# A planner that follows every engine decides which side work stands between the products

## The chip, the cores and the metric

One Trainium2 chip, one of its cores. The metric is the device time of one execution in microseconds (us), shorter being better. A core has a matrix engine (TensorE, PE in the rows; its weight loads are PEld), a vector engine (VectorE, DVE), a scalar engine (ScalarE, ACT) and GpSimd (POOL). SyncE (SP) issues the DMAs. Each engine works through its own list of instructions in order; semaphores tie the lists together. TensorE writes to PSUM, which has eight banks here, and the others read it from there.

## The reference

Attention over four batches and eight heads, then two gated feed-forward layers, in the reference's own types (the weights are 64-bit floats).

```python
# attention: q_l, k_l, v_l (4, 8, 512, 64); q_g, k_g, v_g (4, 8, 32, 64)
out_g = sm(scale * q_g @ k_all.T) @ v_all                 # 32 global rows see all 544
s_l = concat(scale * q_l @ k_g.T, where(|i - j| <= 32, scale * q_l @ k_l.T, -1e9))
out_l = sm(s_l) @ concat(v_g, v_l)                        # a band of 65, and the global keys
x = concat(out_g, out_l) as (2176, 512)
# layer 1: RMS norm, SiLU gate, d_ff 1536
xn = x / sqrt(mean(x * x) + 1e-6) * rms_g
y = (silu(xn @ w_gate) * (xn @ w_val)) @ w_out
# layer 2: sigmoid gate, weights of its own
out = (sigmoid(y @ w2_gate) * (y @ w2_val)) @ w2_out
```

## The kernel before

The 2176 rows are 17 tiles of 128 rows: 16 local tiles T = 0 to 15 and a last one of the four batches' global rows, called xG. They are kept in three parts q = 0, 1, 2 of 6, 6 and 5 tiles, as a high and a low half in f16 (`xhi`, `xlo`). The feed-forward layers are cut into 12 blocks g of 256 hidden columns: g = 0 to 5 are layer 1, g = 6 to 11 layer 2. Every product of f32 accuracy is three products of f16 (high by high, high by low, low by high).

**Attention** is a list `steps` of small steps: `st_q` and `st_k` turn the tile's queries and keys (four transposes each, ScalarE copies), `st_a1` writes a band mask and the scores into two PSUM banks (L809 and L816), `st_mx` and `st_ex` make the softmax, `st_a2` turns it (transposes, L747), `st_a3` multiplies by the values (L871), `st_nm`, `st_rm`, `rms_scale` norm it, `st_a4` and `st_a4b` turn it into `xhi` and `xlo`. `st_sg` and `st_g1` to `st_g3` do the global rows. `slot(u)` writes the steps of half a tile in the order of the list `ORDER`, with fixed lags between a tile's steps. Up to step n0 (four steps behind the third tile's `st_a4b`) a fixed plan runs them with the first weights between.

**Blocks 0 to 2** run on "chunks" of three tiles: `gv_mm` (48 products, L311) makes gate and value, `gv_post` multiplies them into `hhi`, `hlo` (t on VectorE at L334 to L340, hhi on ScalarE, hlo on GpSimd), and `out1` (24 products, L499) multiplies by the third weight and adds into `yacc`. Below, "a full product" is one of 128x384 of L311 or L499. `flush()` issues the `out1` of the chunk before, after the first half (24 products) of a chunk. `first` sets the order of the chunks of g = 0 and 1: the two blocks alternate as tiles come ready.

**Blocks 3 to 11** run on the parts q. `quad_gv` needs 7 instead of 8 sub-products of 2x2 blocks, which takes sums of the weights (`sums`) and of x (`x_combos`, `y_combos`; tiles xb, tt). A pair of products fills one of four PSUM pairs `p`, and VectorE adds it into G or V (L421). Block 6 is plain.

**Weights.** A weight n (three per block) is loaded as 64-bit words in two halves (`raw`, three buffers), turned to f32 by ScalarE (L139) and VectorE (a shift L151, the sign L154, the low bits L157), and split into a high half (ScalarE, L187) and a low half (VectorE, L190).

**What sets the order.** `tick(n)` stands behind every group of products. It counts: every `pace[1]`-th tick takes one lump from `w_jobs` (a lump is up to five weight instructions), every second or third one lump of `jobs` (the combos), and attention steps follow a rate from `due`, so that they are spread over the products of g = 0 and 1. `w_need` and `j_need` issue what is still missing when a block begins.

Of the kernel before, what the change touches and what calls it, by code (L numbers as in the profile page):

```python
# [1 line left out]

# [17 lines left out]
def tile_attention_moe_moe(  # L20
# [110 lines left out]
    def w_scale(n):  # L131

        if n >= NPC or not wide:
            return
        words = w_words.setdefault(n, [])
        if len(words) < 2:
            f = f_tile(n)[:, len(words)]
            words.append(raw_t.pop(0))
            nc.scalar.activation(out=f, in_=words[-1][:, :, 1].bitcast(F32), func=AF.Copy, scale=2.0 ** -112)  # L139

    def w_ahead(k):
        while w_pos[0] < min(k, 2 * NPC):
            w_load()

    def w_bits(n, j, k):

# [1 line left out]
        js = range(2) if j is None else [j]
        if k == 0:
            v = u if j is None else u[:, j]  # L150
            nc.vector.tensor_scalar(out=v, in0=v, scalar1=3, scalar2=None, op0=ALU.logical_shift_left)  # L151
        for j in js:
            if k == 0:
                nc.vector.scalar_tensor_tensor(out=u[:, j], in0=w_words[n][j][:, :, 1], scalar=-0x80000000, in1=u[:, j],  # L154
                                               op0=ALU.bitwise_and, op1=ALU.bitwise_or)
            else:
                nc.vector.scalar_tensor_tensor(out=u[:, j], in0=w_words[n][j][:, :, 0], scalar=29, in1=u[:, j],  # L157
                                               op0=ALU.logical_shift_right, op1=ALU.bitwise_or)

    def w_conv1(n):  # L160
        w_ahead(2 * n + (3 if wide else 2))
        w_scale(n)
        w_scale(n)
        if wide:
            w_bits(n, None, 0)

    def w_conv2(n):
        if wide:
            w_bits(n, None, 1)
            w_words.pop(n)  # L170
            w_ahead(2 * n + 5)
            w_scale(n + 1)

    def w_half(n, j):
        w_ahead(2 * n + (j + 3 if wide else 2))
        if wide:
            if len(w_words.get(n, [])) <= j:
                w_scale(n)
            w_bits(n, j, 0)
            w_bits(n, j, 1)  # L180
            w_scale(n + j)
            w_ahead(2 * n + j + 4)
            if j == 1:
                w_words.pop(n)
# [12 lines left out]
    def w_block(g):
        w_done[g] = [False, False]

        def mark(i):  # L200
            w_done[g][i] = True

        jobs = []

        def small(f):

            def f2():
                f()
                w_step()
            return f2  # L210

        def late():
            while w_late:
                w_lo(*w_late.pop())

        def conv(w):
            n = 3 * g + w
            if g < GS:
                return [lambda: (late(), w_half(n, 0)), lambda: w_half(n, 1)]
            return [lambda: (late(), w_conv1(n)), lambda: w_conv2(n)]  # L220

        def plain(w, dst):
            def f():
                hi, lo = dst()
                x = w_f.pop(3 * g + w)
                w_hi(x, hi)
                w_late.append((x, hi, lo))
                w_scale(3 * g + w + 1)
            return f

        if g < GS:
            def alloc():
                w_t[g] = [hp.tile([128, 2, 2, 2, DM], F16, tag="wgv", name="wgv"), None]

            jobs.append(small(alloc))
            for w in range(2):
                jobs += conv(w) + [plain(w, lambda w=w: [w_t[g][0][:, :, w, a] for a in range(2)])]
        else:
            def alloc():
                w_t[g] = [pb[1].tile([128, 2, 2, 7, 256], F16, tag="wc", name="wc", bufs=2), None]  # L240

            jobs.append(small(alloc))
            box = {}

            def sums(w):
                x = w_f[3 * g + w].rearrange("p j (a f) -> p (j a) f", a=2)
                sm = pb[1].tile([128, 3, 256], F32, tag="sm", name="sm")
                box[w] = x, sm
                ES[0].tensor_tensor(out=sm[:, 0], in0=x[:, 0], in1=x[:, 2], op=ALU.subtract)
                ES[1].tensor_tensor(out=x[:, 2], in0=x[:, 2], in1=x[:, 3], op=ALU.add)  # L250

            def sums2(w):
                x, sm = box[w]
                ES[2].tensor_tensor(out=sm[:, 1], in0=x[:, 2], in1=x[:, 0], op=ALU.subtract)
                ES[3].tensor_tensor(out=sm[:, 2], in0=x[:, 1], in1=sm[:, 1], op=ALU.subtract)

            def hi(w, i):
                w_hi(box[w][i], w_t[g][0][:, w, 0, (0, 4)[i]:(4, 7)[i]])

            def lo(w, i):  # L260
                a, b = (0, 4)[i], (4, 7)[i]
                w_lo(box[w][i], w_t[g][0][:, w, 0, a:b], w_t[g][0][:, w, 1, a:b])
                if i == 0:
                    w_f.pop(3 * g + w)

            for w in range(2):
                jobs += conv(w)
                if g == GP:
                    def parts(w=w):
                        return [w_t[g][0][:, w, a, 0:4].rearrange("p (j a) f -> p j (a f)", j=2) for a in range(2)]  # L270
                    jobs.append(plain(w, parts))
                else:
                    jobs += [lambda w=w: sums(w), lambda w=w: (sums2(w), hi(w, 0)), lambda w=w: (lo(w, 0), hi(w, 1)),
                             lambda w=w: (lo(w, 1), w_scale(3 * g + w + 1))]
            if g == GP:
                jobs.append(small(late))
        wgv_done = len(jobs)

        def alloc_o():
            w_t[g][1] = (hp if g < GS else pb[1]).tile([128, 2, 2, DM], F16, tag="wo", name="wo", bufs=2 if g < GS else 3)  # L280

        jobs += conv(2) + [small(alloc_o), plain(2, lambda: [w_t[g][1][:, :, a] for a in range(2)])]
        if g < GS:
            jobs.insert(wgv_done + 1, small(lambda: mark(0)))
        else:
            jobs.insert(wgv_done, small(lambda: mark(0)))
# [977 lines left out]
```

## Time and profile before

| | |
|---|---|
| median of 3 runs | 930.08 us (929.59 to 931.49) |
| the profiled execution | 930.12 us |
| its span, first to last instruction | 928.3 us |
| TensorE busy | 884.2 us, 95% of the span |
| VectorE, ScalarE, GpSimd busy | 644.8, 373.9, 298.3 us |
| mean granted clock of TensorE | 0.982 of 2.4 GHz |

The profiled execution's own time is 1.8 us over its span and equals the median of the runs. "Busy" counts a matmul from issue to the modelled end of its pipeline, so 95% doesn't mean that only 5% can be had; where matmuls follow each other at a steady pace, the pace is read from the start of one to the start of the next.

### The profile page before, as it was taken

What the parts mean: (1) busy time and instruction counts of PE and PEld (TensorE: products, weight loads), DVE (VectorE), ACT (ScalarE), POOL (GpSimd) and SP (SyncE); (2) the same over time, 40 slices, a digit from 0 to 9 for tenths busy, and PEclk for the clock granted to TensorE, in tenths of its full rate; (3) what the DMA queues carried; (4) which work ended last, traced back from release to release, by engine and by line L of the source; (5) the groups of instructions that cost most, each with busy time, mean ns of one, the idle gap of its engine ahead of it and who ended that gap; (6) DMA issues with size and microseconds to landing.
All of it is one profiled execution on the core that took longest, in us unless ns stands there. A gap on an engine that the chain in (4) does not pass through costs nothing.

```text
span 928.3 us, 19289 instructions
## 1 busy us (share of the span) xinstructions
PE 884.2 (95%) x8119; PEld 549.8 (59%) x8119; DVE 644.8 (69%) x907; ACT 373.9 (40%) x713; POOL 298.3 (32%) x344
## 2 busy tenths in 40 slices
PE   7678889999997999999999799999999999999998
PEld 4556566666674667666666466656556555556553
DVE  2967676446477787899957977738598566997352
ACT  3766666354453342343423444434344223423120
POOL 5544424223256661223221453242122203112120
PEclk9879999999997999999999999999999999999999
DMA  9987874331012111211201211101122011200102
GB/s 193 233 181 153 174 180 99 74 72 25 4 47 90 47 46 46 91 46 46 92 1 46 86 51 46 46 1 47 46 90 92 1 46 46 91 24 1 68 23 102
DMA packets 94183, 67.19 MB, mean 72 GB/s; under 512 B 59280, under 2 KB 84368, under 8 KB 94096
## 3 DMA queue, kind: packets, MB, share of 16 engines
q1 hardware_dynamic: 94096, 65.95, 26.8%
q8 instruction: 64, 1.05, 0.5%
q14 instruction: 23, 0.19, 0.1%
HBM read 52.17 MB, written 4.46 MB: 61 GB/s over the span
## 4 chain that ended last, share of the span: by engine, by line
PE 82%; DVE 10%; issue 3%; ACT 2%; DMA 1%; POOL 1%; SPq 1%; DVEq 0%; POOLq 0%; ACTq 0%
PE p L364 29%; PE p L521 13%; PE b L311 13%; PE p L499 7%; PE b L499 6%; PE p L462 5%; PE b L747 3%; PE b L816 2%; DVE wf L154 2%; PE b L871 2%; DVE wf L157 1%; DVE wf L151 1%; DVE G L421 1%; PE b L789 1%; DMA raw<-in_moe_w_gate_dram 1%
## 5 line engine op out<-in xcount | busy, mean ns | idle before, releaser
L364 PEld LDWEIGHTS <-wc 128*128 128x128 f16 x2016 | 197.4, 98 | 121.1 <-DVE G L421 4.8
L364 PE MATMUL p<-tt,wc 128*128 128x384 f16 (+1 forms) x1152 | 202.0, 319 | 5.9 <-DVE G L421 5.4
L364 PE MATMUL p<-xhi,wc 128*128 128x384 f16 (+1 forms) x576 | 156.3, 317 | 0.0
L401 POOL TENSOR_TENSOR h<-V,h 128x768 f16<-128x768 f32 (+1 forms) x48 | 80.4, 1696 | 235.5 <-ACT h L398 218.3
L311 PE MATMUL b<-xhi,wgv 128*128 128x384 f16 (+1 forms) x576 | 143.0, 319 | 0.0
L521 PE MATMUL p<-wo,h 128*128 128x512 f16 x612 | 133.4, 379 | 0.0
L499 PEld LDWEIGHTS <-wo 128*128 128x128 f16 x864 | 85.2, 99 | 58.4 <-issue 10.9
L311 PEld LDWEIGHTS <-wgv 128*128 128x128 f16 x864 | 83.2, 98 | 45.8 <-issue 1.9
L521 PEld LDWEIGHTS <-h 128*128 128x128 f16 x612 | 59.8, 98 | 71.1 <-POOL h L401 0.2
L311 PE MATMUL b<-xlo,wgv 128*128 128x384 f16 (+1 forms) x288 | 91.6, 318 | 0.4 <-DVE xlo L921 0.4
L364 PE MATMUL p<-xlo,wc 128*128 128x384 f16 (+1 forms) x288 | 91.4, 317 | 0.0
L481 DVE SCALAR_TENSOR_TENSOR ya<-p,ya 128x768 f32<-128x768 f32 (+3 forms) x42 | 42.3, 1017 | 60.6 <-PE p L521 48.2
L499 PE MATMUL b<-hhi,wo 128*128 128x384 f16 (+1 forms) x288 | 76.0, 330 | 7.4 <-ACT hhi L342 4.9
L428 ACT ACTIVATE sa<-p 128x384 f32<-128x384 f32 (+1 forms) x48 | 22.5, 469 | 132.7 <-PE p L364 119.9
L343 POOL TENSOR_TENSOR hlo<-t,hhi 128x384 f16<-128x384 f32 (+1 forms) x36 | 38.5, 1068 | 109.0 <-ACT hhi L342 109.0
L398 ACT ACTIVATE h<-V 128x1536 f16<-128x1536 f32 (+1 forms) x24 | 33.9, 1413 | 93.5 <-DVE V L397 93.5
L499 PE MATMUL p<-h,wo 128*128 128x384 f16 (+1 forms) x432 | 67.3, 317 | 0.0
L421 DVE TENSOR_TENSOR V<-p,V 128x768 f32<-128x768 f32 (+3 forms) x72 | 56.6, 787 | 12.1 <-PE p L364 9.3
L421 DVE TENSOR_TENSOR G<-p,G 128x768 f32<-128x768 f32 (+3 forms) x72 | 56.6, 785 | 8.6 <-PE p L364 6.2
L139 ACT ACTIVATE wf<-raw 128x512 f32<-128x512 f32 x72 | 48.4, 674 | 16.6 <-DMA raw<-in_moe_w_gate_dram 14.3
L157 DVE SCALAR_TENSOR_TENSOR wf<-raw,wf 128x512 int32<-128x512 int32 x72 | 53.8, 779 | 0.6
L154 DVE SCALAR_TENSOR_TENSOR wf<-raw,wf 128x512 int32<-128x512 int32 x72 | 52.4, 758 | 1.6
(137 smaller groups left out, 1296.0 us busy)
## 6 DMA issues: line engine op xcount, KB each, us to landing
raw<-in_moe_w_gate_dram SPq DMA_DIRECT2D x24, 512.0 KB, 4.0
raw<-in_moe_w_val_dram SPq DMA_DIRECT2D x24, 512.0 KB, 4.2
raw<-in_moe_w_out_dram SPq DMA_DIRECT2D x24, 512.0 KB, 3.9
vw<-vt SPq DMA_DIRECT2D x28, 260.0 KB, 5.1
k<-in_k_l_dram SPq DMA_DIRECT2D x16, 256.0 KB, 5.3
q<-in_q_l_dram SPq DMA_DIRECT2D x16, 256.0 KB, 4.5
vt<-in_v_l_dram SPq DMA_DIRECT2D x32, 128.0 KB, 5.0
out_dram<-ya SPq DMA_DIRECT2D x16, 256.0 KB, 2.3
```

The costliest lines, as they stand in the source:

```text
L139: nc.scalar.activation(out=f, in_=words[-1][:, :, 1].bitcast(F32), func=AF.Copy, scale=2.0 ** -112)
L154: nc.vector.scalar_tensor_tensor(out=u[:, j], in0=w_words[n][j][:, :, 1], scalar=-0x80000000, in1=u[:, j], op0=ALU.bitwise_and, op1=ALU.bi ...
L157: nc.vector.scalar_tensor_tensor(out=u[:, j], in0=w_words[n][j][:, :, 0], scalar=29, in1=u[:, j], op0=ALU.logical_shift_right, op1=ALU.bit ...
L311: nc.tensor.matmul(p[:, 0:n], wgv[:, j, gv, a, k * 128:(k + 1) * 128], x[xi][:, k, o:o + n], start=(i == 0), stop=(i == 11),)
L343: EH[3].tensor_tensor(out=lo, in0=t, in1=hi, op=ALU.subtract)
L364: nc.tensor.matmul(p, wc[:, w, a, wi, kt * 128:(kt + 1) * 128], r, start=(i == 0), stop=(i == 5))
L401: EH[j // 2].tensor_tensor(out=lo[:, i:i + 2], in0=vj[:, i - j:i - j + 2], in1=hi[:, i:i + 2], op=ALU.subtract)
L421: nc.vector.tensor_tensor(out=o, in0=p, in1=i, op=ALU.add)
L462: nc.tensor.matmul(gv[:, w], wc[:, w, a, c, (k % 2) * 128:(k % 2 + 1) * 128], x[q][:, k, h * n:(h + 1) * n], start=(i == 0), stop=(i == 11))
L481: nc.vector.scalar_tensor_tensor(out=ya, in0=p, scalar=1.0 / WS, in1=ya, op0=ALU.mult, op1=ALU.add)
L499: nc.tensor.matmul(p[:, i, 0:n], wo[:, j, a, d * 128:(d + 1) * 128], hh[:, j, ho:ho + n], start=(c == 0), stop=(c == 6 * len(gr) - 1),)
L521: nc.tensor.matmul(p[:, i], hh[:, j, (i0 + i) * 128:(i0 + i + 1) * 128], wo[:, j, a, :], start=(c == 0 and g == gr[0]), stop=(c == 5 and g ...
```

## The change

Every call to an engine goes through `Booked`, which issues it as before and also books it: an account holds when each engine is free (`now`), when each tile is written (`wrote`) and when a buffer is free again (`free0`), at costs written in the code. `tick` becomes two loops. `go_on` issues attention steps as long as the account says that the inputs of the next one are there. `give` issues single weight and combo instructions (`c_ops`, `s_ops`, `jobs`), the one due first ahead, while the account says that inputs are ready and the engine is less than `SLACK` (1 us; `ATT`, 0.5 us, during attention) behind TensorE. The lumps, `pace`, `due` and `MARGIN` are gone; `w_need` and `j_need` stay.

Four edits stand beside it: the chunks of block 0 all run before those of block 1 (`first`); once attention is over, `out1` is issued behind the second half of the next chunk (48 products) instead of the first; `st_sg` moves up in `ORDER`; the mask products take 64 rows (as the scores do) instead of 32, and their GpSimd set-up shrinks. The number of full products, quads, weights and sums is the same.

```diff
+    def book(key, outs, ins, cost, lat, port=False):
+        t = max([now[key]] + [wrote.get(tag_of(x), 0.0) for x in ins] + [free0.get(x.tensor.name, 0.0) for x in outs])
+        if port:
+            t = max(t, now["port"])
+            now["port"] = t + cost
+        now[key] = t + cost
...
+                    if key == "d":
+                        c = 75 + (0.52 if sb and len(data) < 2 and "axis" not in kw else 1.04) * n
+                    elif key == "a":
+                        c = 100 + 0.83 * n + 90 * (kw.get("bias") is not None) + 190 * ("accum_out" in kw)
...
+    EARLY = {"e": 100, "d": 500, "a": 500, None: 0}
+
+    def go_on():
+        while pos[0] < len(steps):
+            e, ins = needs(*steps[pos[0]])
+            t = max([0.0] + [wrote.get(tile_name(x), 0.0) for x in ins])
+            if t > now["e"] + EARLY[e]:
+                return
+            run_to(pos[0] + 1)
...
+    def fits(key, op):
...
+        sl = SLACK if pos[0] == len(steps) else ATT
+        t = max(now["e"], now[e]) + sl
+        if now[e] > now["e"] + sl or ins and any(wrote.get(tag_of(x), 0.0) > t for x in ins()):
+            return False
+        return free or ready.get(key, 0) <= t
...
     def tick(n):
-        pace[0] += 1
-        if jobs and pace[0] % pace[2] == 0:
-            i = min(range(len(jobs)), key=lambda i: (jobs[i][0][1], i))
-            jobs.pop(i)[1]()
-        if pace[0] % pace[1] == 0:
-            w_step()
-        t0 = clock[0]
-        clock[0] = t1 = t0 + n
-        if t0 < due[-1][0]:
-            rate = max((s - clock[1]) / (c - t0) for c, s in due if c > t0)
-            clock[1] += max(rate, 0.0) * n
-            run_to(int(clock[1]))
-
+        go_on()
+        give()
...
-    first = [(0, 0, 3), (0, 3, 3), (1, 0, 3), (1, 3, 3), (0, 6, 3), (1, 6, 3), (0, 9, 3), (1, 9, 3), (0, 12, 3), (0, 15, 2), (1, 12, 3), (1, 15, 2)]
...
+    first = [(0, 0, 3), (0, 3, 3), (0, 6, 3), (0, 9, 3), (0, 12, 3), (0, 15, 2), (1, 0, 3), (1, 3, 3), (1, 6, 3), (1, 9, 3), (1, 12, 3), (1, 15, 2)]
...
                 gv_mm(g, ch, j, 1)
+                if j == 1 and wi < len(work) - 1:
+                    flush()
                 gv_post(g, ch, j)
                 tick(ch[2])
-                if j == 0 and wi < len(work) - 1:
+                if j == 0 and wi < len(work) - 1 and pos[0] < len(steps):
                     flush()
...
-    ORDER = ['g1', 'a1', 'k', 'a2', 'mx', 'sc', 'q', 'g1x', 'sg', 'a3', 'a4', 'ex', 'a4b', 'nm', 'rm', 'g']
+    ORDER = ['g1', 'a1', 'sg', 'k', 'a2', 'mx', 'sc', 'q', 'g1x', 'a3', 'a4', 'ex', 'a4b', 'nm', 'rm', 'g']
```

Three places show what moves. In the changed kernel every booked instruction carries the line of the wrapper, L111. The first is TensorE in the attention of tile 10. Before, one step (four transposes of a tile's softmax, `s`) stands between groups of six full products of block 1:

```order
L311 MATMUL b_2428<-xhi0_73,wgv_1486 128x384
L747 MATMUL b_2495<-ident_82,s_2294 128x128 x4
L311 LDWEIGHTS wgv_1486
L311 MATMUL b_2504<-xhi0_73,wgv_1486 128x384
L311 LDWEIGHTS wgv_1486
L311 MATMUL b_2504<-xlo0_76,wgv_1486 128x384
```

In the changed kernel the steps behind the scores of tile 10 follow each other (transposes of s, q, the products by the values, transposes of x), and the next full product is one of block 0's `out1`:

```order
L111 MATMUL b_2537<-ident_82,s_2395 128x128 x4
L111 MATMUL b_2546<-ident_82,q_2142 128x128 x4
L111 MATMUL b_2555<-vw1_89,pt_2448 32x65 x16
L111 MATMUL b_2572<-ident_82,x_2268 128x128 x4
L111 LDWEIGHTS wo_1132
L111 MATMUL b_2583<-hhi_1579,wo_1132 128x384
```

From the scores of tile 5 to the transposes of xG, which are the last of attention, 606 full products stand on TensorE before and 234 after; tiles 9 to 15 have 366 and 84 of them. The attention steps between are the same. The 372 products moved behind attention.

The second place is VectorE where the sums of x and the weights meet the `t` of `gv_post`. Before, between two `t` in a row, thirteen instructions stand:

```order
L334 SCALAR_TENSOR_TENSOR t_4574<-b_4559,t_4574 128x384
L151 TENSOR_SCALAR wf_2310<-wf_2310 128x512
L154 SCALAR_TENSOR_TENSOR wf_2310<-raw_2241,wf_2310 128x512
L157 SCALAR_TENSOR_TENSOR wf_2310<-raw_2241,wf_2310 128x512
L616 TENSOR_TENSOR xb_4579<-xhi0_73,xlo0_76 128x768
L590 TENSOR_TENSOR xb_4579<-xb_4579 128x768
L190 SCALAR_TENSOR_TENSOR wgv_4553<-wf_2310,wgv_4553 128x2x512
L151 TENSOR_SCALAR wf_4584<-wf_4584 128x512
L154 SCALAR_TENSOR_TENSOR wf_4584<-raw_2312,wf_4584 128x512
L157 SCALAR_TENSOR_TENSOR wf_4584<-raw_2312,wf_4584 128x512
L590 TENSOR_TENSOR xb_4579<-xb_4579 128x384
```

(three more weight instructions, and then the next `t`). In the changed kernel a like place has nine, none of them a sum of x:

```order
L111 SCALAR_TENSOR_TENSOR t_4130<-b_4115,t_4130 128x384
L111 SCALAR_TENSOR_TENSOR wf_4064<-raw_3865,wf_4064 128x512 x2
L111 TENSOR_SCALAR wf_4064<-wf_4064 128x512
L111 SCALAR_TENSOR_TENSOR wf_4064<-raw_4044,wf_4064 128x512 x2
L111 TENSOR_SCALAR wf_4177<-wf_4177 128x512
L111 SCALAR_TENSOR_TENSOR wf_4177<-raw_4082,wf_4177 128x512 x2
L111 SCALAR_TENSOR_TENSOR wgv_4181<-wf_4064,wgv_4181 128x2x512
L111 SCALAR_TENSOR_TENSOR t_4214<-b_4149,t_4214 128x384
```

The third is VectorE in the last quad of block 5 (part 2), where layer 2's sums begin. Before, a sum of y (ya) and two weight instructions stand among the additions of G:

```order
L397 SCALAR_TENSOR_TENSOR V<-V,G 128x1536
L421 TENSOR_TENSOR G<-p,sa 128x2x320
L590 TENSOR_TENSOR ya_79<-ya_79 128x768
L157 SCALAR_TENSOR_TENSOR wf<-raw,wf 128x512 x2
L421 TENSOR_TENSOR G<-p,G 128x2x320
L421 TENSOR_TENSOR G<-p,G 128x320
```

In the changed kernel the additions of G follow each other:

```order
L111 SCALAR_TENSOR_TENSOR V<-V,G 128x1536
L111 TENSOR_TENSOR G<-p,sa 128x2x320
L111 TENSOR_TENSOR G<-p,G 128x2x320
L111 TENSOR_TENSOR G<-p,G 128x320
L111 TENSOR_TENSOR G<-p,G 128x2x320
L111 TENSOR_TENSOR ya_79<-ya_79 128x768
L111 TENSOR_TENSOR V<-p,sa 128x2x320
```

The weight instructions stand behind that quad's additions of V now.

## Rows read from the trace of the kernel before

**Rows 1.** The page: engines, and granted clock in 40 slices

```profile
PE 884.2 (95%) x8119; PEld 549.8 (59%) x8119; DVE 644.8 (69%) x907; ACT 373.9 (40%) x713; POOL 298.3 (32%) x344
...
PEclk9879999999997999999999999999999999999999
```

**Rows 2.** Windows between marks of attention: us, busy (x instructions), granted clock, DMA

```profile
17.01:60.50 43.49, 31.03 (x825) 23.50 (x819) 38.08 (x70) 28.23 (x82) 22.80 (x35) 0.84 0.94 215
60.50:110.84 50.34, 42.30 (x933) 30.47 (x930) 31.12 (x64) 32.53 (x99) 21.22 (x42) 0.93 0.84 171
110.84:212.80 101.96, 97.81 (x1646) 65.08 (x1646) 58.98 (x119) 56.82 (x162) 33.41 (x60) 1.00 0.45 104
212.80:251.59 38.79, 38.79 (x523) 25.58 (x523) 22.82 (x54) 15.17 (x37) 12.82 (x20) 1.00 0.07 17
251.59:928.30 676.71, 660.58 (x4044) 396.76 (x4041) 492.68 (x602) 234.25 (x318) 201.00 (x147) 0.99 0.15 52
```

**Rows 3.** Chain that ended last: a stretch of products without a wait

```profile
363.59 27.30 PE p L364 x168
```

**Rows 4.** TensorE's waits, 60.50 to 110.84: total us, times, longest

```profile
PE b L816 <- issue: 2.8, 1, 2.8
PE b L816 <- ACT kT L763: 1.7, 1, 1.7
PE b L747 <- DVE x L891: 1.1, 1, 1.1
PE b L871 <- issue: 0.8, 1, 0.8
PE b L959 <- ACT ptg L944: 0.7, 1, 0.7
PE b L747 <- DVE xlo L921: 0.7, 1, 0.7
PE b L311 <- DVE xlo L921: 0.4, 1, 0.4
```

**Rows 5.** Windows of 5 us in attention

```profile
27.00:32.00 5.00, 5.00 (x124) 3.77 (x124) 4.83 (x9) 4.38 (x16) 1.28 (x3) 0.61 0.65 143
32.00:37.00 5.00, 4.14 (x172) 3.27 (x169) 4.84 (x10) 5.00 (x15) 0.75 (x1) 1.00 1.21 286
...
62.00:67.00 5.00, 2.97 (x64) 2.41 (x66) 3.66 (x7) 2.92 (x12) 3.93 (x7) 0.80 0.93 173
67.00:72.00 5.00, 4.62 (x116) 3.51 (x117) 2.47 (x6) 3.24 (x10) 0.00 (x0) 0.86 0.64 152
```

**Rows 6.** TensorE's waits, 251.59 to 928.30

```profile
PE p L364 <- DVE G L421: 5.4, 3, 4.4
PE b L499 <- ACT hhi L342: 4.9, 2, 3.1
PE b L499 <- POOL hlo L343: 1.0, 2, 0.5
PE p L364 <- DVE V L421: 0.5, 1, 0.5
```

**Rows 7.** Windows around these waits

```profile
262.00:297.00 35.00, 29.26 (x193) 19.42 (x192) 28.62 (x36) 15.84 (x29) 18.52 (x13) 0.90 0.28 90
297.00:363.60 66.60, 66.44 (x430) 42.66 (x430) 49.43 (x72) 24.14 (x43) 39.76 (x32) 0.97 0.15 48
492.00:524.00 32.00, 26.98 (x171) 16.96 (x169) 28.86 (x32) 14.77 (x19) 10.08 (x6) 0.95 0.20 66
```

**Rows 8.** VectorE in order of time: two t of a chunk

```profile
268.27 0.56 DVE L334 SCALAR_TENSOR_TENSOR t<-b,t 128x384 f32<-128x384 f32 x1 [1.34 <-PE b L311]
...
279.69 0.55 DVE L334 SCALAR_TENSOR_TENSOR t<-b,t 128x384 f32<-128x384 f32 x1
```

**Rows 9.** VectorE and GpSimd in order of time, at the longest wait

```profile
513.87 4.17 DVE L157 SCALAR_TENSOR_TENSOR wf<-raw,wf 128x512 int32<-128x512 int32 x2
...
513.73 3.77 POOL L401 TENSOR_TENSOR h<-V,h 128x768 f16<-128x768 f32 x2 [8.84 <-ACT h L398]
```

**Rows 10.** Groups by form: the mask products

```profile
L809 PE MATMUL b<-mask,ident 32*32 32x256 bf16 x128 | 6.8, 290 | 0.0
```

More of the change, by code (lines that the diff above doesn't have):

```diff
@@ L143, in w_ahead, with w_give, w_shift @@
+    w_used = [0]
+    w_go = [False]
+    def w_give():
+        h = hist.get(("stg", "raw"), [])
+        while (wide and w_go[0] and w_pos[0] < 2 * NPC and w_pos[0] - w_used[0] < 3 and now["s"] < now["e"] + 1500
+               and (len(h) < 3 or last.get(h[-3], 0.0) < now["e"] + 500)):
             w_load()
-    def w_bits(n, j, k):
+    def w_shift(n, j):
         u = w_f[n].bitcast(I32)
[L148 to L169, printed above, removed]
[L170 to L184 removed]
+        v = u if j is None else u[:, j]
@@ L190, in w_lo @@
         nc.vector.scalar_tensor_tensor(out=lo, in0=f, scalar=WS, in1=hi, op0=ALU.mult, op1=ALU.subtract)
-    w_jobs = []
-    w_late = []
-    w_done = {}
-    def w_block(g):
-        w_done[g] = [False, False]
[L200 to L208, printed above, removed]
-                w_step()
[L210 to L237, printed above, removed]
-        else:
[L239 to L286, printed above, removed]
-        jobs.append(lambda: (late(), mark(1)))
-        w_jobs.extend(jobs)
@@ new lines, in tile_attention_moe_moe, with due_w, due_j @@
+    starts = {}
+    def due_w(ops):
+        x = ops[0]
+        left = sum(y.g == x.g and (y.w < 2) == (x.w < 2) for y in (*c_ops, *s_ops))
+        return starts.get((x.g, 0) if x.w < 2 else (group[x.g][-1], 1), now["e"] + 50000 * x.g) - STEP * left
+    def due_j(key):
+        q, k = key
+        left = sum(len(x[1]) for x in jobs if x[0] == key)
+        if k == 0:
+            t = starts[GP, q]
+        else:
+            t = min(t for (g, p), t in starts.items() if p == q and g not in (2, GP) and t > now["e"])
+        return t - STEP * left
@@ L575, in outs @@
             h_t.pop((g, key))
+            if key in (2, chunks_b[-1]) or g < 2 and key == last[g]:
+                wo_live.remove(g)
     jobs = []
-    EG = [nc.vector if c == "d" else nc.gpsimd for c in "ddpppppdpd"]
+    EGN = "ddpppppdpd"
+    EG = [nc.vector if c == "d" else nc.gpsimd for c in EGN]
     def combos(q, kt, b):
@@ L640, in tile_attention_moe_moe @@
     gB = const.tile([128, DM], F32, name="gB")
-    masks = [const.tile([128, 128], BF16, name=f"mask{i}") for i in range(3)]
+    mask = const.tile([128, 5, 32], BF16, name="mask")
     qgT = const.tile([128, NPR, B * SG], F32, name="qgT")
```

433 lines of the change are left out of this document (352 added, 81 removed).

## Prediction

> **What bounds the kernel now.** I read the page first, then windows between marks, then what TensorE waited for, then the other engines in order of time at the longest waits. The page shows TensorE at 95% and no other engine above 69% [rows 1], so the reader should ask where TensorE stands still or runs at a lower clock. No product is added or removed; only such losses can change the time.
>
> A price for products first: 168 of them, back to back, take 27.30 us [rows 3], 0.1625 us each for 128x384. The order says how many full products stand between two marks, so the rest of a window is attention with its losses. The marks are the mask of tile 5 (60.50), of tile 9 (110.84), of tile 15 (212.80) and the transposes of xG (251.59) [rows 2]:
> - Tile 5 to 9: 72 full products, 11.7 us of 50.34. Attention with its losses: 38.6 us for 4 tiles, 9.66 each.
> - Tile 9 to 15: 366 products, 59.5 us of 101.96. Attention: 42.5 us for 6 tiles, 7.1 each, at a granted clock of 1.00.
> - Tile 15 to xG: 168 products, 27.3 us of 38.79. Attention: 11.5 us.
>
> So attention is cheap on TensorE where many products stand between its steps, and dearer where few do. The waits of the dear stretch are listed: 4.6 us for ScalarE and VectorE (1.7 + 1.1 + 0.7 + 0.7 + 0.4) and 3.6 us "issue", in which nothing shown was waited for [rows 4]. The mean clock there is 0.93 [rows 2]; in the two windows from 62 to 72, where those for kT and x fall, the clock is 0.80 and 0.86 [rows 5], which is 5 x 0.20 + 5 x 0.14 = 1.7 us.
>
> Behind attention TensorE waits 5.4 + 4.9 + 1.0 + 0.5 = 11.8 us [rows 6], and the clock stands below full in the windows around: 35.0 x 0.10 + 66.6 x 0.03 + 32.0 x 0.05 = 7.1 us [rows 7]. Together 18.9 us. All of it is VectorE coming late, by itself or through ScalarE and GpSimd, which wait for its results.
>
> **The change, part by part.**
>
> *Waits behind attention.* The 4.9 and 1.0 us are `out1` waiting for hhi and hlo. VectorE has 11.4 us between two t (268.27 to 279.69) [rows 8], where TensorE needs 24 x 0.1625 = 3.9 us for the products behind them. Three edits work on this. Weights and sums go out one by one; in the changed order the like place holds 9 weight instructions and no sum of x. `out1` comes 48 products behind its last t, 7.8 us instead of 3.9. And attention ends 372 products earlier in the list, so the sums of x and the weights of blocks 1 to 4 have 372 x 0.1625 = 60.5 us more of products to hide behind. I take these 5.9 us of waits, and the 3.5 + 2.0 us of clock behind them, as gone.
>
> The 5.4 us are additions of G that came late. At the longest, two weight instructions at L157 took 4.17 us while GpSimd had 3.77 us of work on h over the same stretch [rows 9], and the additions of G stood behind them. In the changed order they stand behind that quad's additions of V instead, and the sum of ya behind G's. What that cost VectorE is not removed; it moves to a place where TensorE doesn't wait for it, if the four PSUM pairs give enough slack.
>
> The Trainium skill has a rule for this ("SBUF — State Buffer", the part on engine ports): VectorE with two SBUF inputs and GpSimd lock one port pair for a whole instruction, and the loser waits. The 4.17 us agree with it. By it the conflict goes wherever the two meet, so moving the weights could put it in another quad; that is one reason why I don't count the whole 18.9.
>
> What may stay: bounds 0 (every wait gone) and 18.9 us (none). The account prices VectorE at 75 ns plus 1.04 ns per element and books conflicts, so it lets a little too much through; a wait like the 4.4 us one with part of its clock may come back somewhere. I leave 3 us. **Gain behind attention: 15.9 us.**
>
> *Attention.* This term I am least sure of. From tile 5 to xG 234 full products stand instead of 606: 38.0 us. The account starts a step only when its inputs are (by its own clock) there, but it has little else to issue: block 0 alone feeds it. Per tile, 5 to 15 now hold 14 products (144 for 10 tiles), which is close to tile 5 to 9 before (18), not to 9 to 15 (61). So I start from the near row, 38.6 us for 4 tiles, and take off what a better order could avoid: 4.6 us of waits and the 1.7 us of clock, but not the "issue" waits. That leaves 32.3, **8.1 us per tile**; bounds 7.1 and 9.66. The stretch becomes 10 x 8.1 + 11.5 x 8.1/7.1 + 38.0 = 81 + 13.1 + 38.0 = 132.1 us. Before it took 191.1 us, of which 60.5 moved behind attention at full pace: 130.6. **Attention loses 1.5 us.** ScalarE and VectorE don't bound it at that: their busy time from tile 5 to 9 was 32.5 and 31.1 us for 4 tiles [rows 2], 8.1 and 7.8 per tile with 4 more products each, beside 8.1 + 14 x 0.1625 = 10.4 us.
>
> The Trainium skill speaks against denser attention ("TensorE: Matmul & The Clock Gate", Part 4): transposes don't count as activity for the clock the way products do. Here the trace doesn't follow it: the clock rose from 0.61 to 1.00 between 27 and 37 us, where only attention steps run [rows 5]. By the page the moved-together steps would run at the lower level, and the stretch would come out longer; the trace shows the low clock behind waits.
>
> *First 60 us.* The fixed plan stays; `st_sg` is earlier, one copy of pt stands behind the second tile's value copies on VectorE, and the weights come in half-lumps. VectorE bounds this part (38.08 of 43.49 us [rows 2]) and its instructions are the same. The most to gain is its idle time there, 43.49 - 38.08 = 5.4 us; for a loss I allow as much. Taken as nothing.
>
> *The mask.* 128 mask products are 6.8 us [rows 10], 8 per tile. If the 64-row form runs twice as many side by side it gains up to 3.4 us, if half as many it loses 6.8. I take nothing. GpSimd's shorter set-up lies ahead of the first scores, which wait for loads.
>
> *Sum.* 930.1 - 15.9 + 1.5 = 915.7, so **916 us**. The profiled execution (930.12) is the median of the runs, so no correction is due.
>
> **Rivals.**
> - *Attention stays cheap*, 7.1 us per tile: 71 + 11.5 + 38.0 = 120.5 us, a gain of 10.1; and with it only 1 us of the late waits returns, a gain of 17.9. 930.1 - 28.0 = **902 us**. For it: the account knows each step's inputs and the engines have room. Against: the cheap row had 61 products per tile.
> - *Attention starves TensorE* (the one that ends slower): with few products each wait is bare, the clock falls behind it, and a tile costs 9.66 us, as before between tile 5 and 9: 96.6 + 11.5 x 9.66/7.1 + 38.0 = 150.2 us, a loss of 19.6. 930.1 - 15.9 + 19.6 = **934 us**. It decides from (11.62 x t + 38.0) = 130.6 + 15.9, a tile cost of t = 9.3 us. For it: a measured row with nearly the same mix. Against: 6.3 of its 38.6 us come from the order that the change replaces.
> - *The late waits only move*: VectorE has the same work, and the additions of G wait at other quads for what stood at this one. Then 15.9 us of gain vanish and attention's small loss stays: **931 us**, about as before.
>
> **How the numbers follow.** Forecast 0.57 (908 to 925), attention cheap 0.22, starved 0.15, waits moved 0.06. Under 0.2% (1.9 us) a measurement of this kernel can't tell from no change. The last case spreads around no change: 0.01 faster, 0.05 the same. Faster: 0.57 + 0.22 + 0.01 = 0.80. Slower: 0.15. Same: 0.05. The range must leave out no more than 0.2: it reaches down to the cheap case, 901, and up to just below the starved one, 931.
>
> **What would show it.** The windows of the changed kernel should show 132 us between the masks of tile 5 and the transposes of xG, at a clock of 0.93 to 1.00; then no wait of TensorE over 3 us up to the end, the `out1` of blocks 1 and 2 without waits for hhi, and a clock of 1.00 in the stretch where the sums of x are made. L157 beside GpSimd's h may still take 4 us for two; TensorE should not wait behind it. Wrong would be: masks 12 us apart and more with waits for ScalarE in between (starved), or additions of G named in waits of several us (moved).

## The result and the profile after

The changed kernel takes **921.06 us** (median, 920.17 to 922.31), the kernel before 929.84 (928.73 to 931.49) beside it: a ratio of **0.9905 [0.9884, 0.9926]**. The profiled execution took 920.17 us, its span is 918.3. Three executions below were far slower than all others of the same kernel (1231 us of e5, 3179 us of e12, 1513 us of the kernel before beside e11 to e13), and the ranges and ratios leave them out.

The windows of the changed kernel, between the same marks as [rows 2]: the masks of tiles 1, 4, 5, 9 and 15, the transposes of xG (198.65) and the end. The columns are us, busy time (x instructions) of PE, PEld, DVE, ACT and POOL, granted clock, DMA share and GB/s.

```profile
17.66:54.96 37.30, 23.84 (x592) 18.98 (x592) 28.11 (x52) 22.52 (x70) 20.25 (x33) 0.76 0.92 195
54.96:68.68 13.72, 7.52 (x230) 6.11 (x229) 8.31 (x17) 4.72 (x12) 2.48 (x3) 0.75 0.53 118
68.68:116.11 47.43, 40.34 (x918) 29.53 (x917) 28.97 (x63) 31.49 (x98) 21.76 (x44) 0.90 0.77 166
116.11:170.21 54.10, 50.78 (x1364) 38.52 (x1364) 34.84 (x75) 38.25 (x120) 23.21 (x47) 1.00 0.77 165
170.21:198.65 28.44, 26.72 (x450) 18.14 (x445) 18.90 (x45) 17.27 (x47) 12.39 (x21) 1.00 0.11 25
198.65:918.30 719.65, 714.52 (x4416) 431.70 (x4413) 512.93 (x645) 250.72 (x354) 210.11 (x158) 1.00 0.16 52
```

Three stretches make the span, and the prediction had a number for each (its first 60.5 us unchanged; 676.71 + 60.5 - 15.9 = 721.3 for the last):

| stretch | before | predicted | after |
|---|---|---|---|
| start to the mask of tile 5 | 60.5 | 60.5 | 68.7 |
| tile 5 to the transposes of xG | 191.1 | 132.1 | 130.0 |
| from there to the end | 676.7 | 721.3 | 719.65 |
| span | 928.3 | 913.9 | 918.3 |

Two come out 2 us better than predicted. The first is 8.2 us worse. What TensorE waited for in the last stretch of the changed kernel (total us, times, longest) is all that answers to [rows 6]:

```profile
PE p L111 <- DVE ya L111: 0.5, 1, 0.5
PE p L111 <- DVE V L111: 0.3, 1, 0.3
```

The 8.2 us stand in front of tile 5. Here is the changed kernel in order of time: SyncE's queue (SPq), ScalarE, VectorE and TensorE (start, duration, instruction, and in brackets the idle time before it and what ended it).

```profile
48.51 1.13 SPq L111 DMA_DIRECT2D raw<-in_moe_w_out_dram  x1
58.45 0.37 SPq L111 DMA_DIRECT2D q<-in_q_l_dram  x1
58.92 0.64 SPq L111 DMA_DIRECT2D raw<-in_moe_w_out_dram  x1
...
47.06 0.66 ACT L111 ACTIVATE wf<-raw 128x512 f32<-128x512 f32 x1 [4.42 <-DMA raw<-in_moe_w_val_dram]
65.31 0.66 ACT L111 ACTIVATE wf<-raw 128x512 f32<-128x512 f32 x1 [3.92 <-DMA raw<-in_moe_w_out_dram]
...
66.00 0.43 DVE L111 TENSOR_SCALAR wf<-wf 128x512 int32<-128x512 int32 x1 [5.04 <-ACT wf L111]
...
68.68 0.61 PE L111 MATMUL b<-mask,ident 64*32 64x256 bf16 x8 [6.20 <-DVE x L111]
```

Read it from the bottom. TensorE waits 6.20 us for x of an attention tile. VectorE makes that x behind a weight instruction, for which it had stood 5.04 us. That one waited for ScalarE's conversion, and ScalarE for a raw half of the weights, which SyncE issued only at 58.92: its queue stood from 49.64 to 58.45 in front of a load of q, until TensorE had transposed an earlier q, and the raw half was behind that. Before 47.06 ScalarE had waited 4.42 us for another raw half. The code says why the load is so late. In the fixed plan of the changed kernel, a raw half is loaded when its conversion is issued and none is there:

```python
if x.eng == "a" and ops is c_ops and not raw_t:
    w_load()
```

The loads ahead of need are left to `give`, which doesn't run in the fixed plan. Before, every conversion issued the load of a later half (`w_ahead`). This is one of two edits that the whole loss needs; the other is the new place of `st_sg` (e6).

### The profile page after: what moved, and what is told of

It is laid out like the page before. It is cut to its first block, busy times and chain, and to the rows that moved or that the text cites. A ratio compares the mean times of both kernels' runs of the same rounds, so it can differ in the third digit from the quotient of the medians.

```text
span 918.3 us, 19229 instructions
## 1 busy us (share of the span) xinstructions
PE 877.1 (96%) x8119; PEld 551.3 (60%) x8119; DVE 633.8 (69%) x897; ACT 371.7 (40%) x713; POOL 294.4 (32%) x328
## 4 chain that ended last, share of the span: by engine, by line
PE 89%; DVE 4%; DMA 2%; ACT 2%; issue 2%; SPq 1%; POOL 0%; ACTq 0%; DVEq 0%; POOLq 0%
PE p L111 58%; PE b L111 30%; DVE wf L111 1%; SPq L111 1%; DMA raw<-in_moe_w_val_dram 1%; DMA raw<-in_moe_w_out_dram 1%; ACT pt L111 1%; DMA vg<-in_v_g_dram 0%; DVE xlo L111 0%; DVE vw L111 0%; DVE G L111 0%; DMA x<-in_k_g_dram 0%; DVE ya L111 0%; DVE x L111 0%; ACT kT L111 0%
## 5 line engine op out<-in xcount | busy, mean ns | idle before, releaser
L111 PEld LDWEIGHTS <-wc 128*128 128x128 f16 x2304 | 225.3, 98 | 130.9 <-issue 0.7
L111 PE MATMUL p<-xhi,wc 128*128 128x384 f16 (+1 forms) x768 | 200.8, 317 | 0.5 <-DVE ya L111 0.5
L111 PE MATMUL p<-tt,wc 128*128 128x384 f16 (+1 forms) x1152 | 200.5, 317 | 0.3 <-DVE V L111 0.3
L111 POOL TENSOR_TENSOR h<-V,h 128x768 f16<-128x768 f32 (+1 forms) x48 | 76.7, 1620 | 265.3 <-ACT h L111 265.3
L111 PE MATMUL b<-xhi,wgv 128*128 128x384 f16 (+1 forms) x576 | 138.6, 318 | 0.7 <-ACT xhi L111 0.7
L111 PE MATMUL p<-wo,h 128*128 128x512 f16 x612 | 133.4, 379 | 0.0
L111 PE MATMUL p<-xlo,wc 128*128 128x384 f16 (+1 forms) x384 | 121.7, 317 | 0.0
L111 DVE SCALAR_TENSOR_TENSOR wf<-raw,wf 128x512 int32<-128x512 int32 x144 | 113.9, 800 | 2.2
L111 PEld LDWEIGHTS <-wgv 128*128 128x128 f16 x864 | 84.3, 98 | 49.1 <-issue 2.6
L111 PEld LDWEIGHTS <-wo 128*128 128x128 f16 x864 | 84.5, 98 | 47.8 <-issue 0.4
L111 PEld LDWEIGHTS <-h 128*128 128x128 f16 x612 | 59.9, 98 | 71.0
L111 PE MATMUL b<-xlo,wgv 128*128 128x384 f16 (+1 forms) x288 | 91.6, 318 | 0.6 <-DVE xlo L111 0.6
L111 DVE SCALAR_TENSOR_TENSOR ya<-p,ya 128x768 f32<-128x768 f32 (+3 forms) x42 | 42.3, 1017 | 63.2 <-PE p L111 63.0
L111 ACT ACTIVATE h<-V 128x1536 f16<-128x1536 f32 (+3 forms) x30 | 36.9, 1231 | 97.5 <-DVE V L111 97.5
L111 ACT ACTIVATE sa<-p 128x384 f32<-128x384 f32 (+1 forms) x48 | 22.6, 471 | 126.2 <-PE p L111 104.0
L111 PE MATMUL b<-hhi,wo 128*128 128x384 f16 (+1 forms) x288 | 69.9, 317 | 0.0
L111 ACT ACTIVATE wf<-raw 128x512 f32<-128x512 f32 x72 | 47.5, 671 | 53.7 <-DVE wc L111 25.4
L111 POOL TENSOR_TENSOR hlo<-t,hhi 128x384 f16<-128x384 f32 (+1 forms) x36 | 37.3, 1036 | 96.7 <-ACT hhi L111 96.7
L111 PE MATMUL p<-h,wo 128*128 128x384 f16 (+1 forms) x432 | 67.3, 317 | 0.0
L111 DVE TENSOR_TENSOR V<-p,V 128x768 f32<-128x768 f32 (+3 forms) x72 | 56.5, 785 | 11.6 <-PE p L111 9.0
L111 DVE TENSOR_TENSOR G<-p,G 128x768 f32<-128x768 f32 (+3 forms) x72 | 56.5, 784 | 7.5 <-PE p L111 5.6
L111 DVE TENSOR_SCALAR wf<-wf 128x1024 int32<-128x1024 int32 (+1 forms) x45 | 31.2, 693 | 27.2 <-ACT wf L111 27.0
```

What stands on the lines that cost most here:

```text
L111: return f(*args, **kw)
```

## The experiments

Each kernel was timed against the kernel before on the same chip, which took 930.6 to 931.4 us beside them. All keep the whole computation.

A number used below is the **loss behind attention**: the window from the transposes of xG to the end, less what it would take without waits and at full clock. The prediction's reading of before gives that as 676.71 - 18.9 us; it grows by 0.1625 us [rows 3] for each full product fewer than 606 that the program has between tile 5 and xG. For the changed kernel, with 234: 657.8 + 372 x 0.1625 = 718.3, and its loss is 719.65 - 718.3 = 1.4 us.

### The late raw halves

**e1: the changed kernel with raw halves loaded ahead in the fixed plan.**

```diff
         w_used[0] += 1
+        if wide and not w_go[0]:
+            w_load()
```

Expected: 

> The changed kernel, but in the fixed plan of the first 60 us a raw half is loaded as soon as one has been used up, as the kernel before did. Theory (a raw half is loaded only when its conversion is issued, so ScalarE stands 4.4 and 3.9 us for it and attention behind it): no wait of ScalarE for a raw half over 1 us before 70 us, the mask of tile 5 at 60 to 62 us instead of 68.7, time 921 - 8 = 913 us. Rival (the new step order or the mask products slowed the first tiles): the mask of tile 5 stays at 67 to 69 us, 921 us.

Measured: **912.82 us** (911.82 to 913.6), ratio 0.9792 [0.9776, 0.9809]. The load that was issued at 58.92 is now issued at 43.96, and ScalarE's conversion has no wait before it. Rows of e1 in order of time:

```profile
43.96 0.35 SPq L111 DMA_DIRECT2D raw<-in_moe_w_out_dram  x1
...
59.28 0.71 ACT L111 ACTIVATE wf<-raw 128x512 f32<-128x512 f32 x1
...
62.70 0.49 PE L111 MATMUL b<-mask,ident 64*32 64x256 bf16 x8 [2.42 <-DVE x L111]
```

The mask of tile 5 comes at 62.70 instead of 68.68, just above the 60 to 62 that were expected. The stretches behind it take 130.1 and 719.0 us, as in the changed kernel. So nearly all of the gain in the spans (918.3 to 911.8) is where the theory puts it, and 2.2 of the 8.2 us remain. That the late loads alone made the 8.2 us doesn't follow: e6 takes back nearly as much with the loads still on demand. This version beats both kernels.

**e7: the kernel before with the raw halves of block 0 loaded on demand.**

```diff
+            if not raw_t:
+                w_load()
...
-        w_ahead(2 * n + (j + 3 if wide else 2))
+        if n >= 3:
+            w_ahead(2 * n + (j + 3 if wide else 2))
...
-            w_scale(n + j)
-            w_ahead(2 * n + j + 4)
+            if n >= 3:
+                w_scale(n + j)
+                w_ahead(2 * n + j + 4)
...
-                w_scale(3 * g + w + 1)
+                if 3 * g + w >= 2:
+                    w_scale(3 * g + w + 1)
```

The last two pieces also take out the conversions that were issued ahead in block 0 (`w_scale`), so the edit is a little more than the loads alone.

Expected: 

> The kernel before, with one part of the change alone: in block 0 a raw half is loaded only when its conversion is issued. Theory: the first tiles get as late as in the changed kernel, mask of tile 5 at 67 to 69 us instead of 60.5; before's attention is spread over products, so part of it may be caught up: 934 to 938 us. Rival (step order, mask): 930 us, tile 5 at 60 to 61 us.

Measured: 936.36 us (934.45 to 939.65), ratio 1.0054 [1.0038, 1.0070]. ScalarE of e7 now waits, where before it had one wait of 1.20 us:

```profile
43.24 0.66 ACT L141 ACTIVATE wf<-raw 128x512 f32<-128x512 f32 x1 [2.52 <-DMA raw<-in_moe_w_val_dram]
...
66.57 0.67 ACT L141 ACTIVATE wf<-raw 128x512 f32<-128x512 f32 x1 [2.81 <-DMA raw<-in_moe_w_gate_dram]
...
83.93 0.66 ACT L141 ACTIVATE wf<-raw 128x512 f32<-128x512 f32 x1 [4.06 <-DMA raw<-in_moe_w_gate_dram]
```

Late raw halves cost in the old schedule too, some 5 us, as the theory has it; but only 2.1 of them lie ahead of tile 5 (62.62), the rest behind it. The mark at 67 to 69 us that the theory expected did not come: with the old step order, late halves delay tile 5 little.

### The small edits

**e4: the old masks of 32 rows and their set-up in the changed kernel.**

```diff
-                r = slice(64 * e, 64 * e + 64)
...
-                    one[r, 64 * e:64 * e + 32],
-                    mask[r, x:x + 2].unsqueeze(1).to_broadcast([64, NPR, 2, 32]),
...
+                r = slice(32 * i, 32 * i + 32)
...
+                nc.tensor.matmul(two(p[r].rearrange("p r (a c) -> p r a c", c=32)), one[r, r],
```

Expected: 

> The changed kernel with the 32-row mask products and their longer set-up on GpSimd. The trace shows eight mask products at 0.30 us in the 64-row form and 0.40 in the 32-row form, 16 times: the mask accounts for 0 to 2 us, so 921 to 923 us. Rival (the 64-row form delays the scores behind it): 1 us or more faster than the changed kernel.

Measured: 921.36 us (919.75 to 926.23), ratio 0.9893 [0.9861, 0.9925]: the mask makes no difference, as predicted. In the changed kernel the group of mask products reads

```profile
L111 PE MATMUL b<-mask,ident 64*32 64x256 bf16 x128 | 5.7, 295 | 8.6 <-DVE x L111 6.2 <-ACT s L111 2.4
```

against 6.8 us in [rows 10]. The profiled execution of e4 was its slowest (926.23); from tile 5 to xG it took 136.1 us, against 130.0 in the changed kernel. One profile of that stretch is good to some 6 us, no better. The mask of tile 5 is steadier: in the five runs that have the changed kernel's first part (itself, e2, e4, e10, e13) it comes at 67.6 to 68.9 us.

**e2 and e5: the place of out1.** e2 is the changed kernel with `out1` behind the first half again:

```diff
-                if j == 1 and wi < len(work) - 1:
-                    flush()
...
-                if j == 0 and wi < len(work) - 1 and pos[0] < len(steps):
+                if j == 0 and wi < len(work) - 1:
                     flush()
```

Expected: 

> The changed kernel with out1 behind the first half of the next chunk all along, as before the change; all else as changed. If the later place is what removed TensorE's waits for hhi and hlo (5.9 us) and the low clock behind them (3.5 + 2.0 us), several of these microseconds come back: 925 to 932, with hhi or hlo among TensorE's waits behind attention. If the account's one-by-one issue and the moved products removed them by themselves: 921 within 1.5, and no such wait.

Measured: 921.39 us (915.74 to 922.67), ratio 0.9889 [0.9850, 0.9928]. From xG to the end it takes 719.66 us, where the changed kernel takes 719.65, and no wait for hhi stands there: the second case. e5 makes the edit the other way round, alone, in the kernel before:

```diff
+                if j == 1 and wi < len(work) - 1 and pos[0] == len(steps):
+                    flush()
...
-                if j == 0 and wi < len(work) - 1:
+                if j == 0 and wi < len(work) - 1 and pos[0] < len(steps):
                     flush()
```

Expected: 

> The kernel before the change with only this edit: once attention is over, out1 comes behind the second half of the next chunk. If the later place alone is enough: the 5.9 us of waits and up to 5.5 us of clock go, 920 to 926. If the lumps of weights and sums still hold VectorE up for longer than the added 3.9 us: 929 to 932, with waits for hhi left.

Measured: 929.72 us (926.64 to 931.86), ratio 0.9987 [0.9970, 1.0004], again the second case. The wait for hhi shrinks from 4.9 to 2.8 us, that for G stays at 5.4:

```profile
PE p L364 <- DVE G L421: 5.4, 3, 4.4
PE b L499 <- ACT hhi L342: 2.8, 2, 2.1
```

So the later `out1` is worth some 1 us in the old schedule (by the interval, at most 3), and nothing in the new one.

### Room, account, or both

**e12: the kernel before with only the new order of chunks.** Block 0 runs ahead of block 1; 318 full products stand between tile 5 and xG instead of 606, so 288 of the 372 move behind attention.

```diff
-    first = [(0, 0, 3), (0, 3, 3), (1, 0, 3), (1, 3, 3), (0, 6, 3), (1, 6, 3), (0, 9, 3), (1, 9, 3), (0, 12, 3), (0, 15, 2), (1, 12, 3), (1, 15, 2)]
+    first = [(0, 0, 3), (0, 3, 3), (0, 6, 3), (0, 9, 3), (0, 12, 3), (0, 15, 2), (1, 0, 3), (1, 3, 3), (1, 6, 3), (1, 9, 3), (1, 12, 3), (1, 15, 2)]
```

Expected: 

> The kernel before the change with only the new order of chunks: all of block 0 ahead of block 1, so that attention ends earlier and more products stand behind it; lumps and paces as before. If the room behind attention alone removes the late sums and weights: 915 to 920, with the waits for hhi and G gone. If the account is needed to make use of the room (the lumps go by a count of ticks): 925 to 932, with waits for G of 3 us and more left.

Measured: 930.86 us (928.99 to 932.91), ratio 1.0001 [0.9985, 1.0016], the second case. TensorE's waits of e12 from xG (207.94) on are much like those of [rows 6]:

```profile
PE p L364 <- DVE G L421: 5.4, 3, 4.4
PE b L499 <- ACT hhi L342: 5.3, 2, 3.5
PE b L499 <- POOL hlo L343: 1.3, 2, 0.7
```

Room alone does nothing: the lumps go by a count of ticks and stand where they stood. VectorE's first sum of x starts 6.6 us behind xG's transposes in both (258.19 before, 214.53 in e12). The loss behind attention is 721.96 - 704.6 = 17.4 us.

e12 also settles a side effect of the room. Behind attention, `gv_post` makes a `t` with one VectorE instruction (L334), during attention with two (L338, L340). VectorE has 907 instructions before, 897 in the changed kernel and 899 in e12: most of that saving is in e12 too, and it gains nothing.

**e8: the account without the room.** This is e1 with the products of block 1 back between the attention steps (612 from tile 5 to xG) and with one attention step at most at a time. That limit was not tried alone.

```diff
-    first = [(0, 0, 3), (0, 3, 3), (0, 6, 3), (0, 9, 3), (0, 12, 3), (0, 15, 2), (1, 0, 3), (1, 3, 3), (1, 6, 3), (1, 9, 3), (1, 12, 3), (1, 15, 2)]
+    first = [(0, 0, 3), (0, 3, 3), (1, 0, 3), (1, 3, 3), (0, 6, 3), (1, 6, 3), (0, 9, 3), (1, 9, 3), (0, 12, 3), (0, 15, 2), (1, 12, 3), (1, 15, 2)]
...
             run_to(pos[0] + 1)
+            return
...
-            if wi + 1 == len(work) or work[wi + 1][0] != g:
+            if all(w[0] != g for w in work[wi + 1:]):
```

Expected: 

> The changed kernel with the raw halves ahead (912.8) and with the products of block 1 back between the attention steps: the old alternation of blocks 0 and 1, and one attention step per group of products at most. If packing attention costs next to nothing, as the forecast has it (1.5 us): 910 to 916. If the price of an attention tile follows the products between its steps (7.1 us with 61 of them, against 9.2 now), some 9 us are gained: 903 to 906.

Measured: 946.51 us (942.06 to 946.86), ratio 1.0159 [1.0126, 1.0193]. Neither theory had that. The windows of e8, between the same marks, and TensorE's first two waits behind xG:

```profile
63.02:118.49 55.47, 50.08 (x979) 35.26 (x979) 39.41 (x82) 39.21 (x113) 24.06 (x46) 0.91 0.83 182
118.49:220.90 102.41, 97.13 (x1634) 65.32 (x1634) 60.38 (x123) 53.06 (x152) 34.99 (x59) 0.98 0.46 111
220.90:260.71 39.81, 36.68 (x494) 23.73 (x494) 19.96 (x45) 14.14 (x35) 9.22 (x16) 0.91 0.07 17
260.71:944.40 683.69, 658.08 (x4037) 395.72 (x4035) 474.37 (x589) 231.69 (x316) 193.72 (x147) 0.98 0.15 48
```

```profile
PE p L111 <- DVE ya L111: 16.3, 2, 15.7
PE p L111 <- DVE G L111: 4.4, 2, 3.8
```

The stretch behind xG loses 683.69 - (657.8 - 6 x 0.1625) = 26.9 us, more than the kernel before. One wait is 15.7 us long; its cause is shown at e14, where it is longer still. With less room the account lets three of the six sets of sums of x out in time; the other three are issued together when block 3 begins, from 354.89 on.

The same windows answer the question of what a tile of attention costs. From tile 5 to xG, less the products, e8 has 197.7 - 612 x 0.1625 = 98.2 us, the changed kernel 130.0 - 234 x 0.1625 = 92.0, e12 146.6 - 318 x 0.1625 = 94.9, before 191.1 - 98.5 = 92.6. Spreading the steps among more products makes attention no cheaper; differences of 6 us are within what one profile is good for.

### The margin

The margin says how far an engine may be behind TensorE for the account to issue more work on it (`SLACK`, 1 us, once attention is over).

```diff
-    SLACK = 1000
+    SLACK = 8000
```

**e10: 8 us.** Expected: 

> The changed kernel with the margin that an engine may be behind TensorE once attention is over set from 1 to 8 us, so that the account holds hardly anything back. If holding back is what keeps VectorE in time behind attention: waits for G, V, hhi or ya return, 924 to 932. If the room behind attention (372 more products, out1 later) does it: 920 to 923.

Measured: 1025.66 us (1023.68 to 1026.79), ratio 1.102 [1.0984, 1.1057]. TensorE's waits of e10 behind xG, the three largest:

```profile
PE p L111 <- DVE G L111: 23.6, 10, 4.7
PE p L111 <- ACT sa L111: 14.6, 8, 2.4
PE p L111 <- DVE V L111: 11.0, 7, 3.0
```

The direction is that of the first case, the loss many times its size. The last stretch takes 823.0 us, 103 more than the changed kernel's. Holding back is what keeps the engines in time.

**e13: 2 us** (`SLACK = 2000`). Expected: 

> The changed kernel with the margin behind attention at 2 us instead of 1 (at 8 us: 1025.7). If the account's price is exact enough that only large margins harm: 920 to 923. If each added microsecond of margin goes over into waits for G, V and hhi at many quads: 925 to 940.

Measured: 925.89 us (922.36 to 931.64), ratio 0.9950 [0.9926, 0.9975]. The time is just in the second case's range, but the waits behind attention stand at five places only, 4.3 us in all. The last stretch takes 723.7 us, 4.0 more.

**e14: 0.5 us, on top of e1** (`SLACK = 500`). Expected: 

> The changed kernel with the raw halves ahead (912.8) and the margin behind attention at 0.5 us instead of 1, as a try for a still faster version and the other side of the margin (2 us: 925.9, 8 us: 1025.7, both without the raw halves ahead). Behind attention only some 1 us of loss is left at 1 us, so at best 911 to 913. If the account then holds work back until a block begins and it is issued in a row in front of TensorE's next need, as in the row of sums of 4.8 us: 917 to 930.

Measured: 955.15 us (951.99 to 957.04), ratio 1.0269 [1.0236, 1.0302]: the direction of the second case, with more than twice its size. The last stretch takes 757.06 us. VectorE of e14 at the start of block 3, and TensorE's next product:

```profile
360.00 0.96 DVE L111 TENSOR_TENSOR xb<-xhi,xlo 128x768 f32<-128x768 f16 x1 [4.30 <-POOL tt L111]
362.48 1.55 DVE L111 TENSOR_TENSOR xb<-xb 128x768 f32<-128x768 f32 x2 [1.52 <-POOL xb L111]
368.33 0.83 DVE L111 TENSOR_TENSOR xb<-xhi,xlo 128x640 f32<-128x640 f16 x1 [4.29 <-POOL tt L111]
...
378.84 3.27 DVE L111 SCALAR_TENSOR_TENSOR ya<-b,ya 128x384 f32<-128x384 f32 x8
...
381.50 0.48 PE L111 MATMUL p<-xhi,wc 128*128 128x384 f16 x1 [24.41 <-DVE ya L111]
```

Four of the six sets of sums of x are issued in a row from 351.05 on, each set on VectorE waiting for GpSimd to finish the one before. Behind them stand the eight additions into ya that empty PSUM, and TensorE waits 24.41 us for those. All of this work existed before; held back too long, it meets the point where a block needs it.

### The place of st_sg

**e6: the old ORDER in the changed kernel.**

```diff
-    ORDER = ['g1', 'a1', 'sg', 'k', 'a2', 'mx', 'sc', 'q', 'g1x', 'a3', 'a4', 'ex', 'a4b', 'nm', 'rm', 'g']
+    ORDER = ['g1', 'a1', 'k', 'a2', 'mx', 'sc', 'q', 'g1x', 'sg', 'a3', 'a4', 'ex', 'a4b', 'nm', 'rm', 'g']
```

Expected: 

> The changed kernel with the old ORDER list (st_sg behind g1x). Theory of the late raw halves: tile 5 stays within 2 us of 68.7 and the time within 2 us of 921. Rival (the step order costs the first tiles): tile 5 at 60 to 63 us, 913 to 915 us.

Measured: 928.60 us (925.43 to 932.78), ratio 0.9977 [0.9952, 1.0002]. The time fits neither case, but the mark does not stay at 68.7, as the theory of the late raw halves had it; it comes near the rival's 60 to 63:

```profile
63.45 0.60 PE L111 MATMUL b<-mask,ident 64*32 64x256 bf16 x8 [3.87 <-DVE x L111]
```

The raw halves are still loaded on demand here, and ScalarE waits 3.90 and 1.73 us for two of them.

**e11: the same edit on top of e1.** Expected: 

> The changed kernel with the raw halves ahead (912.8) and the old place of st_sg in ORDER. With the raw halves on demand the old ORDER cost 7.5 us, of which 5.1 were one wait for sums of x issued in a row at the start of block 3. If the old ORDER itself costs that: 917 to 921. If that wait was a chance product of where the account stood: 912 to 915.

Measured: 923.26 us (922.45 to 924.09), ratio 0.9926 [0.9898, 0.9954], 10 us above e1 and above both cases. The mask of tile 5:

```profile
61.11 0.49 PE L111 MATMUL b<-mask,ident 64*32 64x256 bf16 x8 [2.42 <-DVE x L111]
```

So four kernels give the mask of tile 5 for each pair of the two edits:

| mask of tile 5, us | raw halves on demand | raw halves ahead |
|---|---|---|
| new place of `st_sg` | 68.68 (changed kernel) | 62.70 (e1) |
| old place | 63.45 (e6) | 61.11 (e11) |

Against 61.11, either edit alone costs 1.6 to 2.3 us, both together 7.6. With the raw halves ahead, e8 and e14 have the mark at 63.02 and 64.27, so only the corner with both edits stands clear of the scatter. The 8.2 us are mostly the work of the two together; how they add up on the queues was not followed.

Undoing the place of `st_sg` costs more behind attention than it saves in front. TensorE waits in both for ya at the start of block 3, 5.1 us in e6 and 4.8 in e11, the wait of e8 and e14 with fewer sums in the row. The rows of e6 and e11:

```profile
PE p L111 <- DVE ya L111: 5.1, 1, 5.1
```

```profile
PE p L111 <- DVE ya L111: 4.8, 1, 4.8
```

With 258 products between tile 5 and xG the loss behind attention is 724.31 - 714.4 = 9.9 us in e6 and 724.51 - 714.4 = 10.1 in e11. So the line in `ORDER`, which I had costed at nothing by itself, decides some 9 us behind attention; about half of it is that one wait, some 150 us later. That it comes about through where the account stands then is the likely reading, not a shown one.

## Why the prediction was right and where it was wrong

The time lay 5 us above the forecast and in its range; the mechanism forecast is the one that happened. By its steps:

- ***First 60 us*: the step that failed.** "VectorE bounds this part (...) and its instructions are the same. (...) Taken as nothing", with 5.4 us either way. It cost 8.2. The bound was VectorE's idle time, and a wait for a load isn't bounded by that. The loss needs two things that the prediction prices at nothing: raw halves that are loaded on demand, which it doesn't mention, and the earlier `st_sg`, which it does. Undoing the first takes 6.0 of the 8.2 us back (e1, and with them 8.2 us of the median), undoing the second 5.2 (e6). Seeing the first would have needed the place of the raw halves on SyncE's queue in the fixed plan, before and after. In the old schedule the late halves cost 5 us, but only 2.1 of them ahead of tile 5 (e7).
- *Waits behind attention*: 17.5 of the 18.9 us went (predicted 15.9), and both the wait for hhi and the 4.4 us one for G are gone. Of the three edits that the prediction names, the later `out1` had no part in it (e2, e5). Neither of the other two is enough alone: room without the account loses 17.4 us (e12), the account without room 26.9 (e8), both 1.4. Nor are both always enough: with nearly the same room and the old place of `st_sg` the account loses 10 (e6, e11).
- *Attention*: 130.0 us against 132.1, which is t = (130.0 - 38.0) / 11.62 = 7.9 us per tile where 8.1 was taken; the starved case, from 9.3, was far off. But the reasoning behind it does not hold. "Attention is cheap on TensorE where many products stand between its steps" was read from tiles 9 to 15, at 61 products each. In the changed kernel those tiles have 14 and cost (54.10 - 84 x 0.1625) / 6 = **6.7 us** each, cheaper than the 7.1 of before. Tiles 5 to 9 cost (47.43 - 60 x 0.1625) / 4 = **9.4**, about the 9.66 of before. The price follows the tile's place in time, at a clock of 0.90 and 1.00, and not the products between. The windows above say what it is made of. In the early stretch TensorE is idle for 47.43 - 40.34 = 7.1 us and the clock costs some 47.43 x 0.10 = 4.7, by the prediction's way of counting; in the late one it is idle for 54.10 - 50.78 = 3.3 us at full clock. Without these a tile costs 6.5 us early and 6.2 late. The early tiles come close to the sign given for starvation: their masks stand 47.43 / 4 = 11.9 us apart. The mean of early and late happens to be near the 8.1 that I took; that is luck. Why the waits and the low clock stand in the early tiles wasn't tried.
- Denser attention does not bring a low clock here either: the granted clock is 1.00 from 116.11 to 170.21, where the steps of six tiles stand with 84 full products. What the Trainium skill states ("TensorE: Matmul & The Clock Gate", Part 4) is about transposes, and those are some 20 of the 50.8 us that TensorE is busy there and 2.6 of 9.1 between 27 and 37 us in [rows 5]. So neither stretch tests that statement, and "the trace doesn't follow it" in the prediction says too much.
- *The mask* as nothing: right (e4).
- *The late waits only move* had 0.06. It didn't happen in this version, but it is close by: one line of `ORDER` or half a microsecond of margin brings waits of 5 to 24 us back (e6, e11, e14). The prediction could price the waits from the rows; that the planner would get the margin right could not be read from the trace.

## What to carry to other kernels

A planner that issues work "when its inputs are ready" also has to issue the loads behind those inputs early, in every phase of the program; check the DMA issues of the phase that the planner does not cover. When a planner holds work back, look for the place where all that is left is issued at once: the cost is not in the mean but in the one row in front of a block. When undoing one edit takes a loss back, undo the others too: here two edits made the loss together, and each experiment alone seemed to have found its cause. And a price read from two stretches that differ in several things (here, in place and in products between) should not be put down to one of them.

## What the hardware showed unexpectedly

TensorE has waits in which nothing that the profile shows was waited for ("issue"), 10.5 us in all in the changed kernel, and the longest recurs at nearly the same place of the program, among the scores of tile 7. Here it is in the changed kernel, then in e4, in e1 and in the kernel before:

```profile
93.72 0.63 PE L111 MATMUL b<-kT,qT 64*32 64x128 f32 x20 [3.16 <-issue]
```

```profile
95.12 1.07 PE L111 MATMUL b<-kT,qT 64*32 64x128 f32 x20 [3.48 <-issue]
```

```profile
87.46 0.63 PE L111 MATMUL b<-kT,qT 64*32 64x128 f32 x22 [1.81 <-issue]
```

```profile
86.04 0.67 PE L816 MATMUL b<-kT,qT 64*32 64x128 f32 x13 [2.77 <-issue]
```

A tile has 64 of these products; the wait stands in front of the last 20, 20, 22 and 13 of them.

Of the 10.5 us, 7.7 lie between tile 5 and xG, where the DMA share is about 0.77 up to 170 us, and the rest ahead of tile 5; behind attention, at 0.16, there are none. The page lists two small DMA queues of the kind "instruction" beside the big one. Whether these waits are instructions that arrive late among the loads was not tried.
